# Wider fillers, earlier zeros and a new written order in a delta-rule and mixture-attention kernel

## The chip, the cores and the metric

The kernel runs on 1 core of one Trainium2 chip. The metric is the device time in microseconds (us); lower is better. The engines have short names: PE is TensorE (PEld its weight load), DVE is VectorE, ACT is ScalarE, POOL is GpSimd, SP is SyncE, which issues all transfers here.

## The reference

Two layers follow each other. The first is a linear recurrence (the delta rule) over 768 tokens for 4 x 8 heads of width 48; its output is the input of the second, four softmax-attention experts of width 64 with top-2 gating.

```python
k_n = k / (np.linalg.norm(k, axis=-1, keepdims=True) + 1e-06)
for t in range(S):
    kt, vt, bt = (k_n[:, :, t], v[:, :, t], beta[:, :, t, None])
    y[:, :, t] = np.einsum('bhd,bhde->bhe', q[:, :, t], state)
    v_old = np.einsum('bhde,bhd->bhe', state, kt)
    state = state + bt[:, :, :, None] * np.einsum('bhd,bhe->bhde', kt, vt - v_old)
...
for e in range(E):
    q = x @ wq[e]
    k = x @ wk[e]
    v = x @ wv[e]
    scores = scale * (q @ k.transpose(0, 2, 1))
    scores = np.where(causal, -1000000000.0, scores)
    a = softmax(scores)
    ye = a @ v @ wo[e]
    out += (weight of e for each token, 0 unless e is in its top 2) * ye
```

## The kernel before

The recurrence is done in blocks of 64 tokens. A chunk, numbered n from 0 to 5, holds two of the four batch entries, all heads and 256 tokens, in four parts c of 64 tokens; chunks 0 to 2 are one half of the batch from first to last token, chunks 3 to 5 the other. For each chunk the Gram matrices of its keys are formed (ga for chunks 0 to 2, gb for 3 to 5) and evacuated by ACT (ge, ad, ae, al). Norms are taken (nm), the blocks are turned round (bi), and a 32 x 32 triangular system is solved by substitution: chunk 0 on DVE (the steps s0.1 to s0.31), the others on POOL (sv.n.0 to sv.n.31; sv.n.32 is on DVE). bo and tn transpose the solution, m1, we, m2 and me join two solved halves into the inverse of a 64 x 64 block. Then the parts follow one after another, since each needs the state behind the one before: gk (products of keys with keys and state), xs (values less their old part, DVE), tx (solve), us (copies), ku (state update), se (the new state), yy (outputs), yh and yl (outputs split in two words). hx moves some rows of the outputs with six transfers. The second layer is made of pj, pv (projections), mx, mz, mr, mt, mo (row maxima), sc (scores), sm (mask), ex (exponentials), av (values), gt (gating), ra, rb, nr (normalising), ft and fo (output projection), oo and so (storing). It runs some chunks behind the recurrence, between its matmuls.

Nothing is scheduled by a compiler. The string ORDER is the program: each word is a step, with the numbers of its chunk and part behind dots and its accumulator banks behind "@", and every engine runs its own instructions of these words in that order. The words that load are lk (keys), lq (queries), lt and lv (keys and values by token), le (keys for the Gram matrices), lc (constants; lc.1 is beta), ww (weights, staged in one of two places and then split by wh on ACT and wl on POOL; the place is free for a later ww only when wl is done). SP issues them in the order of their words and waits in place where a buffer isn't free. vs scales the values by the norms on POOL.

fl.k is a filler: k matmuls on a tile of zeros, ZB, into a bank that nothing reads, so that PE is not idle while it waits. zb zeroes ZB. zz and zb also zero states and two banks. ex0 and sq0 are activations whose only use is that ACT switches its table there.

```python
for word in ORDER.split():
    word, _, at_ = word.partition("@")
    name, *a = word.split(".")
    ...
    steps[name](*a)
```

An fp32 matmul of the recurrence counts as two instructions on PE; a filler counts as one. Nearly all matmuls carry the line of the helper mm, L199, and nearly all copies on ACT that of copy, L201.

## Time and profile before

| | us |
|---|---|
| median of 3 runs | 426.77 (424.69 to 426.94) |
| profiled execution | 421.56 |
| its span | 419.8 |

| engine | busy us | share | instructions |
|---|---|---|---|
| PE | 399.7 | 95% | 9119 |
| DVE | 302.8 | 72% | 635 |
| ACT | 205.7 | 49% | 453 |
| POOL | 227.0 | 54% | 415 |

The times are those of whole runs; the span is the time from the first to the last instruction of the one execution that was profiled, and 1.76 us lie around it. Busy time counts fillers like any other matmul. In rows of the trace, the time behind an operation's start is the busy time of the group, xN is the number of instructions, and brackets tell how long the engine had been idle before it and what ended that.

### The profile page before, as it was taken

The numbers are of one execution on the slowest core, as the hardware profiler recorded it, in microseconds if no ns is written. First come the engines' busy times: TensorE is split into PE (matmuls) and PEld (weight loads), VectorE is DVE, ScalarE is ACT, GpSimd is POOL, SyncE is SP. The second block draws the span as 40 slices with busy tenths as digits, with TensorE's granted clock in tenths as the row PEclk, the third lists the DMA queues.
The fourth block names the chain that finished last, engine by engine and source line by source line (L and its number), as shares of the span: only waits on it lengthen the run. The fifth ranks groups of instructions, "written<-read, shape, count | busy, mean of one in ns | idle before, by whom it ended". The sixth has DMA issues, their size and how long they took to land.

```text
span 419.8 us, 20613 instructions
## 1 busy us (share of the span) xinstructions
PE 399.7 (95%) x9119; PEld 356.3 (85%) x9119; DVE 302.8 (72%) x635; ACT 205.7 (49%) x453; POOL 227.0 (54%) x415
## 2 busy tenths in 40 slices
...
GB/s 212 244 125 132 6 61 90 199 87 174 53 153 141 140 69 58 77 142 154 213 56 43 94 21 108 103 120 4 160 173 125 52 20 13 11 16 62 4 3 75
DMA packets 81657, 39.81 MB, mean 95 GB/s; under 512 B 64992, under 2 KB 74848, under 8 KB 81568
## 3 DMA queue, kind: packets, MB, share of 16 engines
...
q8 instruction: 71, 1.16, 1.1%
q14 instruction: 18, 0.15, 0.1%
...
## 4 chain that ended last, share of the span: by engine, by line
PE 73%; DVE 10%; DMA 8%; SPq 3%; issue 3%; ACT 1%; POOL 1%; DVEq 0%; ACTq 0%
PE p L199 71%; DMA bt<-in_beta_dram 2%; DVE p L460 2%; DMA qp<-in_kq_dram 2%; DVE vs L459 1%; SPq L637 1%; DVE mp L730 1%; DMA at<-in_wqk_dram 1%; PE p L814 1%; DVE qp L395 1%; DMA kv<-in_kv_dram 1%; DMA at<-in_wo_dram 1%; PE p L739 1%; DVE p L725 1%; POOL wl L312 1%
## 5 line engine op out<-in xcount | busy, mean ns | idle before, releaser
L508 POOL TENSOR_TENSOR tm<-b 128x30 f32<-128x30 f32 (+9 forms) x150 | 72.9, 486 | 28.9 <-DVE b L504 18.1
L510 POOL TENSOR_TENSOR b<-b,tm 128x30 f32<-128x30 f32 (+9 forms) x150 | 77.7, 518 | 11.8
L199 PE MATMUL p<-zb 128*128 128x128 bf16 x883 | 55.9, 222 | 4.5 <-DVE zb L316 3.3
L775 ACT ACTIVATE at<-p 128x768 f32<-128x768 f32 (+1 forms) x48 | 43.3, 917 | 31.4 <-PE p L199 14.8
L199 PEld LDWEIGHTS <-zb 128*128 128x128 bf16 x883 | 50.7, 99 | 6.5 <-DVE zb L316 3.3
L201 ACT ACTIVATE qp<-p 64x192 f32<-64x192 f32 (+1 forms) x92 | 36.9, 401 | 26.0 <-PE p L199 24.6
L730 DVE TENSOR_REDUCE mp<-p 128x2 f32<-128x1024 f32 (+3 forms) x40 | 44.4, 1115 | 2.9 <-PE p L199 1.9
L199 PE MATMUL p<-vs,at 128*64 128x65 f32 x1344 | 44.9, 223 | 0.9 <-ACT at L775 0.9
L199 PEld LDWEIGHTS p<-vs,at 128*64 128x64 f32 x1344 | 41.4, 137 | 4.4 <-issue 2.0
L395 DVE TENSOR_TENSOR qp<-p,cs 64x256 f32<-64x256 f32 x96 | 40.5, 421 | 5.8 <-PE p L199 4.1
L199 PE MATMUL p<-xu,wh 128*128 128x512 f32 (+1 forms) x168 | 40.3, 373 | 0.0
L572 POOL TENSOR_TENSOR kv<-kv,nt 128x384 f32<-128x384 f32 x24 | 19.6, 831 | 31.2 <-DMA kv<-in_kv_dram 25.7
L199 PEld LDWEIGHTS p<-xu,wh 128*128 128x128 f32 x168 | 27.8, 188 | 5.8 <-issue 0.5
L199 PE MATMUL p<-qh,kh 64*128 64x128 f32 (+1 forms) x192 | 29.1, 299 | 0.2 <-DVE mp L730 0.2
L199 PE MATMUL p<-qp 128*48 128x64 f32 (+1 forms) x768 | 26.3, 221 | 2.2 <-issue 1.9
L780 DVE TENSOR_TENSOR p<-p,km 128x512 f32<-128x512 f32 x24 | 16.6, 696 | 14.6 <-PE p L199 14.2
L199 PE MATMUL p<-qh,kl 64*128 64x128 f32 (+1 forms) x192 | 26.9, 276 | 0.0
L199 PE MATMUL p<-ql,kh 64*128 64x128 f32 (+1 forms) x192 | 26.9, 276 | 0.0
L199 PE MATMUL p<-wh,xu 128*128 128x260 f32 x144 | 26.3, 294 | 0.6 <-DVE mp L730 0.6
L199 PEld LDWEIGHTS p<-qp 128*48 128x48 f32 (+1 forms) x768 | 23.0, 123 | 4.5 <-issue 2.8
L199 PE MATMUL p<-mr,sl 64*128 64x128 f32 (+1 forms) x192 | 26.7, 274 | 0.0
L199 PE MATMUL p<-qp,kf 48*64 48x112 f32 (+1 forms) x768 | 23.8, 259 | 0.3 <-issue 0.3
...
## 6 DMA issues: line engine op xcount, KB each, us to landing
...
```

The source lines that it names most:

```text
L199: T.matmul(o, lhsT=a, rhs=b, start=start, stop=True, skip_group_check=True)
L201: copy = lambda o, a: S.activation(o, a, AF.Copy)
L312: G.tensor_tensor(flat(WL[w])[:, i:i + n], st(k)[:, 0:n], flat(WH[w])[:, i:i + n], op=OP.subtract)
L395: V.tensor_tensor(QP[zi(n, c) % RQ][tok(f), f, 4 * x:4 * x + 4, 0:64], gv(n, c)[r, x, :, 0:64], PMK[r, None, :].to_broadcast([64, 4, 64]), ...
L459: V.tensor_tensor(tv, t, l, op=OP.mult)
L460: V.tensor_tensor(PX[:, 0:i, i + 1:], PX[:, 0:i, i + 1:], tv, op=OP.subtract)
L508: G.tensor_tensor(tv, b[:, i:i + 1, i + 1:].to_broadcast([128, i, m]), b[:, 0:i, i:i + 1].to_broadcast([128, i, m]), op=OP.mult)
L510: G.tensor_tensor(b[:, 0:i, i + 1:], b[:, 0:i, i + 1:], tv, op=OP.subtract if n == 1 else OP.add)
L572: G.tensor_tensor(vt, vt, NRM[n % 2][:, c * NP:c * NP + NP, None].to_broadcast([128, NP, HD]), op=OP.mult)
L730: V.tensor_reduce(o[:, :, y0:y0 + per], g, axis=AXL.X, op=OP.max, negate=True)
L775: S.activation(at(n, b, y, kp)[:, :, 0:w], P8[:, b0:b0 + 2, 0:w], AF.Exp, scale=0.125)
L780: V.tensor_tensor(g, g, KM[:, None, None, :].to_broadcast([128, 2, 2, 128]), op=OP.add)
```

## The change

The string ORDER is another one, with the same steps in another sequence, and three things in the steps differ.

- ZB is 512 columns wide instead of 128. A second filler, fw.k, runs k matmuls of 512 columns; fl.k runs k of 128 as before. Counted in the two strings, there were 883 narrow fillers in 30 places and there are 272 narrow and 143 wide ones in 51 words. Before m1.0.0, 487 narrow ones become 57 narrow and 106 wide; behind it, 396 narrow become 215 narrow and 37 wide.
- Zeroing ZB is DVE's first instruction. The memsets of two banks are one, in a word of its own (zp), behind it.
- For chunks 3 to 5 the Gram blocks are addressed through hold(), which describes the same words of GF in rows of 256. (gs has the new name gps.)

The order was searched with another assumption on the time that blocks of the program take while transfers are queued; that search is not part of the kernel. Of the two orders only the lines that are spoken of are shown.

```diff
--- before
+++ after
-lk.0.2 zz.4 zz.0 lk.0.3 lk.0.1 lk.0.0 le.1.3 zz.2 zb le.1.1 zz.5 le.1.0 zz.1 sq0 lc.1 le.1.2 le.2.3 fl.24@3 ga.0.1.1@2
-lc.2 ga.0.1.0@3 al.1.1 ae.1.1.0 le.2.2 ga.0.0.1@4 ae.1.1.3 le.2.0 ae.1.0.0 ae.1.1.1 ae.1.0.1 lq.0.2 ga.0.0.0@5 al.0.1
-ae.1.0.3 ae.0.1.0 lt.0.2 ae.0.1.1 ae.0.0.0 lv.0.1 ae.0.1.3 ae.0.0.1 lt.0.0 ae.0.0.3 lq.0.0 al.1.0 bi.0 fl.25@6
...
-ad.1.1.0.3 ad.1.1.1.0 fl.59@7 ga.2.0.0@2 ad.1.0.0.3 ge.2.1.0 nm.0.3 a2.0 bi.1 ga.2.1.1@6 wh.0 ga.2.0.1@3 ge.2.0.0 s0.8
-gk.0.0@45 a2.1 ge.2.0.1 s0.9 s0.10 s0.11 wh.1 vs.0.0 nm.1.0 s0.12 vs.0.1 ge.2.1.1 nm.1.1 nm.1.2 s0.13 wl.0 s0.14
-sv.1.0 ww.2 gd.2 s0.15 s0.16 s0.17 sv.1.1 sv.1.2 s0.18 wh.2 sv.1.3 lv.0.2 s0.19 ex0 sv.1.4 s0.20 wl.2 s0.21 s0.22 wl.1
-s0.23 vs.0.2 ww.3 s0.24 lk.1.0 sv.1.5 lq.0.1 s0.25 s0.26 sv.1.6 ww.4 s0.27 sv.1.7 s0.28 wh.3 s0.29 sv.1.8 s0.30 s0.31
...
-sv.1.9 sv.1.10 bo.0 sv.1.11 tn.0 tc0.2.1 fl.379@7 m1.0.0@1 sv.1.12 tc0.0.0 m1.0.1@7 tc0.0.1 we.0.0 sv.1.13 we.0.1
-pm.0.0.0.0 fl.14@2 m2.0.0@1 pm.0.0.1.1 m2.0.1@7 pm.0.0.0.1 me.0.0.0 sv.1.14 nm.1.3 tc0.1.0 pm.0.0.1.0 me.0.0.1 tc0.1.1
...
-me.0.2.0 sv.1.27 we.0.3 fl.17@6 tx.0.2@45 sv.1.28 us.0.2.1 le.3.1 sv.1.29 us.0.2.0 le.3.0 lk.1.1 sv.1.30 fl.26@6
-yy.0.2@1 sv.1.31 ku.0.2 yh.0.2.0 yl.0.2.0 wl.3 m2.0.3@4 yh.0.2.1 pj.0.1.0.0@5 se.0.2.1 yl.0.2.1 pj.0.1.0.1 wl.4
-me.0.3.1 ww.5 pj.0.3.0.0@1 me.0.3.0 pj.0.1.0.2 zz.3 sv.1.32 se.0.2.0 ww.6 gb.3.0@23 lv.1.1 le.3.2 vs.1.0 bo.1 lk.1.2
-pv.0.0.1@4 ge.3.0.1 lt.1.0 vs.0.3 ge.3.0.0 pj.0.3.0.1 wh.5 pj.0.3.0.2 tn.1 gk.0.3@23 wl.5 kh.0.3.0 kh.0.1.0 wh.6
...
-lv.5.2 oo.3.1.1 lt.5.2 fl.6@2 ku.5.0 lv.5.1 lv.5.3 yy.5.0@1 se.5.0.0 so.3.1.0 so.3.1.1 pj.4.2.2.0@6 yh.5.0.0 lk.5.3
...
+lk.0.2 zz.4 zb lk.0.3 zp sq0 lk.0.1 lk.0.0 zz.0 lc.1 zz.2 le.1.2 zz.5 le.1.3 le.1.1 ww.0 le.1.0 fl.24@3 ga.0.1.1@2
+lt.0.1 le.2.2 ga.0.1.0@3 al.1.1 le.2.3 ae.1.1.0 le.2.0 ae.1.1.3 ae.1.0.0 lq.0.3 zz.1 ae.1.0.3 fl.12@5 ga.0.0.0@4
+al.1.0 ae.1.0.1 le.2.1 ga.0.0.1@5 lc.2 ae.1.1.1 ae.0.0.0 ae.0.0.1 ae.0.0.3 ae.0.1.0 al.0.0 lv.0.1 ae.0.1.1 lv.0.2
+ae.0.1.3 fw.3@6 fl.7@6 ga.1.1.1@2 lt.0.0 bi.0 lq.0.1 ge.1.1.1 lq.0.0 ad.1.1.1.1 nm.0.0 ad.1.1.1.3 wh.0 nm.0.1 fw.6@6
+fl.4@6 ga.1.0.1@4 px nm.0.2 ga.1.1.0@3 ad.1.0.1.0 ge.1.0.1 s0.1 ga.1.0.0@6 bs s0.2 al.0.1 ad.1.1.0.2 s0.3 ad.1.1.0.0
...
+vs.0.2 s0.12 nm.1.0 gd.2 nm.1.1 nm.1.2 wh.1 wl.2 s0.13 lq.0.2 s0.14 sv.1.0 s0.15 ww.4 s0.16 s0.17 sv.1.1 s0.18 vs.0.0
...
+s0.29 s0.30 s0.31 wl.1 sv.1.10 ww.3 bo.0 sv.1.11 tn.0 tc0.0.0 fw.90@7 fl.4@7 m1.0.0@1 vs.0.1 tc0.2.0 m1.0.1@4 sv.1.12
+m1.0.2@5 we.0.1 we.0.0 nm.1.3 tc0.0.1 fl.9@7 m2.0.0@1 sv.1.13 me.0.0.1 tc0.1.0 sv.1.14 tc0.1.1 me.0.0.0 we.0.2 fw.6@7
+fl.7@7 tx.0.0@23 sv.1.15 m2.0.1@1 us.0.0.1 gk.0.0@45 me.0.1.1 us.0.0.0 sv.1.16 me.0.1.0 lk.1.0 pm.0.0.0.0 tc0.3.1
+fl.4@7 ku.0.0 pm.0.0.1.1 wh.4 pm.0.0.1.0 sv.1.17 m1.0.3@1 se.0.0.0 pm.0.0.0.1 se.0.0.1 we.0.3 fl.10@7 gk.0.1@23
+sv.1.18 ex0 xs.0.1 sv.1.19 pm.0.1.1.1 fw.2@7 fl.5@7 tx.0.1@45 pm.0.1.1.0 pm.0.1.0.0 yy.0.0@1 sv.1.20 pm.0.1.0.1
+us.0.1.0 lq.1.0 bi.2 us.0.1.1 wl.4 tc0.2.1 sv.1.21 fw.3@7 fl.7@7 yy.0.1@4 lk.1.1 yh.0.0.0 lv.1.0 yh.0.0.1 m2.0.3@5
+le.3.1 yl.0.0.1 yh.0.1.0 sv.1.22 yl.0.0.0 ku.0.1 yh.0.1.1 yl.0.1.1 yl.0.1.0 m2.0.2@1 sv.1.23 se.0.1.0 hx.0.0 se.0.1.1
+me.0.2.0 sv.1.24 fl.10@7 gk.0.2@23 tc0.3.0 me.0.2.1 sv.1.25 wh.3 xs.0.2 pm.0.2.0.0 sv.1.26 fw.2@4 fl.5@4 tx.0.2@67
+pm.0.2.1.1 pm.0.2.0.1 le.3.0 us.0.2.1 sv.1.27 pm.0.2.1.0 ww.6 me.0.3.1 us.0.2.0 lv.0.3 sv.1.28 lt.1.0 fw.5@4 fl.7@4
+yy.0.2@1 le.3.2 sv.1.29 lv.1.1 sv.1.30 ku.0.2 lq.1.1 yh.0.2.1 yh.0.2.0 sv.1.31 gb.3.0@23 yl.0.2.1 yl.0.2.0 lq.1.2 wh.6
+me.0.3.0 wl.3 se.0.2.0 pj.0.1.0.0@4 lt.1.1 ge.3.0.0 se.0.2.1 sv.1.32 ww.5 fl.11@6 pv.0.0.1@1 ge.3.0.1 lt.0.3
+pj.0.1.0.1 bo.1 vs.1.1 lg.0.0.1 pj.0.3.0.0@5 pj.0.1.0.2 zz.3 pj.0.3.0.1 wl.6 ve.0.0.1 pj.0.3.0.2 pj.0.2.0.0@1 vs.1.0
...
+gt.3.5 yh.4.1.0 sc.3.1.1.0@23 rb.3.0 gt.3.6 xs.4.2 nr.3.0 yl.4.1.0 lv.5.1 sm.3.1.1 hx.4.0 fl.9@1 tx.4.2@67 sv.5.28
...
@@ -244,7 +245,7 @@
     CS, QM = sb("cs", 209), sb("qm", 128)
     SL = sb("sl", 2, 128, dt=F32R)
     BT = sb("bt", NU, 32)
-    ZB = sb("zb", 128, dt=BF16)
+    ZB = sb("zb", 512, dt=BF16)
     IDN, PMK, LOW, H16 = CS[:, 0:128], CS[:, 128:192], CS[:, 192:208], CS[:, 208:209]
     KM, Z0, HF = sb("km", 128), sb("zr", 32), sb("hf", 1)
     VF = VS.rearrange("p a b c d -> p (a b c d)")
@@ -259,6 +260,9 @@
     PX = P8[:, 0:2].rearrange("p a b -> p (a b)").rearrange("p (j i) -> p j i", i=32)
     AD = AT[0].rearrange("p a b -> p (a b)").rearrange("p (t i) -> p t i", i=32)
 
+    def hold(n, k):
+        return GF[n % RG][:, 16 * k:16 * k + 16].rearrange("p (m t) s -> p m (t s)", m=4)
+
     def zi(n, c):
         return 4 * n + c
 
@@ -314,7 +318,9 @@
 
     def zb():
         V.memset(ZB, 0.0)
-        V.memset(P8[:, 7], 0.0)
+
+    def zp():
+        V.memset(P8[:, 6:8], 0.0)
 
     def ex0():
         S.activation(RS[0][:, 0, 0:1], ZB[:, 0:1], AF.Exp)
@@ -324,8 +330,6 @@
 
     def zz(k):
         if k < 2:
-            if k == 0:
-                V.memset(P8[:, 6], 0.0)
             for i in (k, k + 2):
                 V.memset(zs(i), 0.0)
         elif k == 2:
@@ -343,10 +347,18 @@
 
     def fl(k):
         for _ in range(k):
-            mm(P8[:, BK["fl", k][0], 0:128], ZB, ZB)
+            mm(P8[:, BK["fl", k][0], 0:128], ZB[:, 0:128], ZB[:, 0:128])
+
+    def fw(k):
+        for _ in range(k):
+            mm(P8[:, BK["fw", k][0], 0:512], ZB[:, 0:128], ZB)
 
 
     def le(n, c):
+        if n > 2:
+            nc.sync.dma_start(hold(n, c // 2)[0:112, 2 * (c % 2):2 * (c % 2) + 2],
+                              kq[n, c, 0:112, 0:512].rearrange("p (a b) -> p a b", a=2))
+            return
         nc.sync.dma_start(GF[n % RG][0:112, NP * c:NP * c + NP], kq[n, c, 0:112, 0:512].rearrange("p (a b) -> p a b", a=NP))
 
     def ga(n, k, x):
@@ -362,13 +374,13 @@
     def gb(n, k):
         b = BK["gb", n, k][0]
         for j in range(2):
-            a = GF[n % RG][:, NP * (2 * k + j):NP * (2 * k + j) + NP]
             for i in range(4):
                 for x, f in TURN:
                     p, o = 4 * x + i, 256 * j + 64 * i
-                    mm(P8[gr(f, p), b + x, o:o + 64], a[feat(f), p], a[feat(f), p])
-
-    def gs(n, k, x):
+                    a = hold(n, k)[feat(f), 2 * j + x, 64 * i:64 * i + 64]
+                    mm(P8[gr(f, p), b + x, o:o + 64], a, a)
+
+    def gps(n, k, x):
         g = P8[:, BK["gb", n, k][0] + x] if n > 2 else bank(("ga", n, k, x))
         return g.rearrange("p (c i j) -> p c i j", c=2, i=4)
 
@@ -376,7 +388,10 @@
         return a.rearrange("p (c x i) j -> p c x i j", x=2, i=4)[:, 2 * k:2 * k + 2, x]
 
     def ge(n, k, x):
-        copy(half(GF[n % RG], k, x), gs(n, k, x))
+        if n > 2:
+            copy(hold(n, k).rearrange("p (c x) (i j) -> p c x i j", x=2, i=4)[:, :, x], gps(n, k, x))
+            return
+        copy(half(GF[n % RG], k, x), gps(n, k, x))
 
     def gk(n, c):
         b, a, q = BK["gk", n, c][0], KF[zi(n, c) % RK], QP[zi(n, c) % RQ]
...
```

## Rows read from the trace of the kernel before

**Rows 1.** The page: busy time of each engine with its share of the span and its instructions, and the engines' shares of the chain of work that ended last.
```profile
PE 399.7 (95%) x9119; PEld 356.3 (85%) x9119; DVE 302.8 (72%) x635; ACT 205.7 (49%) x453; POOL 227.0 (54%) x415
...
PE 73%; DVE 10%; DMA 8%; SPq 3%; issue 3%; ACT 1%; POOL 1%; DVEq 0%; ACTq 0%
```

**Rows 2.** Busy time of each engine in two stretches, cut where m1.0.0 starts. Columns: stretch, its length, then busy us and instructions of PE, PEld, DVE, ACT and POOL, the granted clock of PE, the share of the transfer engines and GB/s.
```profile
0.00:46.90 46.90, 41.76 (x905) 40.59 (x905) 37.83 (x94) 18.04 (x39) 32.44 (x53) 1.00 0.64 160
46.90:416.50 369.60, 357.97 (x8216) 315.71 (x8216) 264.98 (x542) 187.15 (x415) 194.60 (x363) 1.00 0.34 86
```

**Rows 3.** The same two stretches for the instructions alone that read or write ZB: PE, PEld, DVE, ACT.
```profile
0.00:46.90 46.90, 29.29 (x487) 28.34 (x487) 0.11 (x1) 0.41 (x2) 1.00 0.64 160
46.90:416.50 369.60, 26.60 (x396) 22.34 (x396) 0.00 (x0) 0.00 (x0) 1.00 0.34 86
```

**Rows 4.** The timeline of the opening: DVE's first memsets, PE's first groups, and the time to landing of the four key loads (min, median, max).
```profile
1.00 0.48 DVE L328 MEMSET p<- 128x512 f32 x1 [1.00 <-PEq L893]
1.64 1.50 DVE L330 MEMSET qp<- 128x768 f32 x2 [0.15 <-issue]
3.10 0.11 DVE L316 MEMSET zb<- 128x64 uint32 x1
...
3.27 2.74 PE L199 MATMUL p<-zb 128*128 128x128 bf16 x24 [3.27 <-DVE zb L316]
5.94 4.54 PE L199 MATMUL p<-kf 48*64 48x64 f32 x128
...
0.82 1.81 SPq L272 DMA_DIRECT2D kf<-in_kq_dram  x4
...
DMA to landing us min/median/max: 2.9/4.0/5.1
```

**Rows 5.** The timeline of DVE, ACT and PE up to m1.0.0: the transpose that opens the first solve, the copy and the square root ahead of DVE's wait, the last transpose (bo.0), the long filler and m1.0.0.
```profile
11.85 1.97 DVE L442 STREAM_TRANSPOSE vs<-at 128x1024 f32<-128x1024 f32 x1 [0.29 <-ACT at L201]
...
26.51 0.63 ACT L201 ACTIVATE wh<-at 128x512 fp32r<-128x512 f32 x1 [0.80 <-DMA at<-in_wqk_dram]
27.05 0.34 ACT L424 ACTIVATE g<-b,hf 128x32 f32<-128x32 f32 x1
...
27.41 0.35 DVE L415 RECIPROCAL rr<-g 128x32 f32<-128x32 f32 x1 [0.39 <-ACT g L424]
...
44.58 2.25 DVE L467 STREAM_TRANSPOSE gf<-vs 128x1024 f32<-128x1024 f32 x1
...
25.14 21.33 PE L199 MATMUL p<-zb 128*128 128x128 bf16 x379
46.89 0.50 PE L199 MATMUL p<-gf,os 32*32 32x32 f32 x19 [0.41 <-DVE gf L467]
```

**Rows 6.** The timeline of POOL's first solve (its first and last instruction), DVE's second transpose behind it, the Gram block gb.3.0 on PE, and m1.1.0 on PE.
```profile
29.48 2.38 POOL L502 TENSOR_TENSOR b<-b,aa 128x1024 f32<-128x1024 f32 x1 [1.49 <-DVE aa L436]
...
69.82 1.27 POOL L512 TENSOR_SCALAR_AFFINE_SELECT b<-b 128x1024 f32<-128x1024 f32 x1
...
76.34 1.92 DVE L470 STREAM_TRANSPOSE tn<-b 128x1024 f32<-128x1024 f32 x1
...
72.97 1.16 PE L199 MATMUL p<-gf 48*64 48x64 f32 x64 [0.96 <-DMA gf<-in_kq_dram]
...
78.98 0.21 PE L199 MATMUL p<-dg,gf 32*32 32x32 f32 x1 [0.83 <-ACT vs L201]
```

**Rows 7.** Whom PE waited for from 46.9 to 416.5 us: total us, times, longest.
```profile
PE p L199 <- issue: 4.6, 5, 1.9
PE p L199 <- ACT at L775: 1.2, 2, 0.9
PE p L199 <- DMA gf<-in_kq_dram: 1.0, 1, 1.0
```

**Rows 8.** The instruction queue on the page (packets, MB, share), and the timeline of PE around its three longest idle times that are put down to "issue".
```profile
q8 instruction: 71, 1.16, 1.1%
...
19.06 2.74 PE L199 MATMUL p<-zb 128*128 128x128 bf16 x46 [1.19 <-issue]
...
105.19 1.00 PE L199 MATMUL p<-qp,kf 48*64 48x112 f32 x32
106.01 0.28 PE L199 MATMUL p<-gf 48*64 48x64 f32 x4
108.01 0.58 PE L199 MATMUL p<-gf 48*64 48x64 f32 x25 [1.72 <-issue]
...
313.32 0.44 PE L199 MATMUL p<-qp 128*48 128x64 f32 x9 [1.92 <-issue]
```

**Rows 9.** The timeline of SP, POOL and PE around the values of chunk 5.
```profile
320.03 1.95 SPq L281 DMA_DIRECT2D kv<-in_kv_dram  x4
...
325.45 0.83 POOL L572 TENSOR_TENSOR kv<-kv,nt 128x384 f32<-128x384 f32 x1 [12.96 <-DMA kv<-in_kv_dram]
...
326.93 0.49 PE L199 MATMUL p<-x,gf 64*64 64x48 f32 x17 [0.79 <-DVE x L575]
```

**Rows 10.** The timeline of ACT: the table switch of ex0, its activation, and a copy of the first recurrence steps with the idle time before it.
```profile
31.51 1.28 ACT L320 ACT_TABLE_LOAD   x1
32.80 0.20 ACT L320 ACTIVATE rs<-zb 128x1 f32<-128x1 bf16 x1
...
57.29 0.28 ACT L201 ACTIVATE h<-p 112x128 fp32r<-112x128 f32 x1 [2.05 <-PE p L199]
```

258 lines of the change are left out of this document (127 added, 131 removed).

## Prediction, made before the changed kernel was run

> **What bounds the kernel now.** The page comes first: TensorE (PE) is busy for 95% of the span, and 73% of the chain that ended last is PE [rows 1]. But 883 of its 9119 matmuls are fillers on zeros, so "busy" is not "useful". The table by stretches cuts the run at 46.9 us, where m1.0.0 starts and the first state can be updated [rows 2], and the same table for the filler operand alone separates the padding [rows 3]. Before the cut PE does 384 useful matmuls and 487 fillers, plus gk.0.0: the pace there is set elsewhere. After it, 369.6 us pass of which PE is busy 357.97, so it idles 11.63 us, and it holds 396 fillers. One filler costs 56 ns when they follow each other: 379 take 21.33 us [rows 5]. So the 396 cost 22.3 us of PE's line. What remains, 369.6 - 11.6 - 22.3 = 335.7 us, is useful matmul work, which the change neither adds to nor takes from; only its order differs. That gives the frame for the sum: the end moves by what the start of m1.0.0 moves, by what the fillers behind it shrink, and by what PE's idle time behind it changes.
>
> The opening shows who sets m1.0.0. VectorE (DVE) runs the 31 steps of the first triangular solve, ends them with the transpose at 44.58 + 2.25 us, and PE, done with 379 fillers, waits 0.41 us for it [rows 5]. GpSimd (POOL) runs the second solve from 29.48 us to the select that ends at 71.1; DVE then needs until 78.3 for the two transposes, and m1.1.0 starts at 78.98 [rows 6]. From there to the end I take PE as the pace setter, with short waits: the list of PE's waits behind 46.9 us names 4.6 us "issue" (nothing that the profile shows), 1.2 for ScalarE's (ACT) exponentials, 1.0 for a transfer [rows 7].
>
> **Edit 1, zeros first.** Today two memsets stand ahead of the one that fillers read: it starts at 3.10 us, and PE's first filler at 3.27 [rows 4]. In the new order it is DVE's first instruction, at about 1.00. It writes four times as much: between 0.11 us (the old one) and 0.44 (four times that), at a time when DVE later sits idle anyway. PE then starts 1.8 to 2.1 us earlier, and its 24 fillers, 2.67 us from first to the next group's start, end near 4.0 instead of 5.94. The first Gram blocks cannot use all of that: they need the first two of four key loads, which land 2.9 to 5.1 us after issue from 0.82 us on [rows 4], so they start at 4.2 to 5.3. Twelve new fillers inside the group take back 0.7 us at 56 ns or 1.3 at the 110 ns of the first fillers, and one state memset, zz.1 (1.5 us, as the pair in [rows 4]), now stands between DVE's copies. Gain at the transpose that starts the solve (11.85 us now): 0 to 0.9 us, I take 0.5.
>
> Further on, DVE idles 0.39 us for the square root of chunk 1, which on ACT queues behind a weight copy that waits for its load [rows 5]. In the new order another copy, wh.2, stands there, with a load issued earlier: 0 to 0.39, I take 0.39. m1.0.0 comes 0.9 us earlier (0 to 1.3). Behind it the POOL solve starts on DVE's result as well, idle 1.49 us for it today [rows 6], so it moves along; its interruptions (vs.0.0, wl.1, vs.0.1, wl.4 against wl.2, wl.1, vs.0.2 before) are nearly equal. **-0.9 us.** The total of zeroed words in the accumulators is unchanged, and the activation-table switch ex0 (1.28 us plus a 0.20 us activation) moves from idle time into the first recurrence steps. There ACT idles 2.05 us at a time today [rows 10], which covers it; uncovered it costs 1.5.
>
> **Edit 2, wide fillers.** Counted in the two orders: before m1.0.0, 487 narrow become 57 narrow and 106 wide; behind it, 396 narrow become 215 narrow and 37 wide. No row shows a wide one. Its bounds: 213 ns (512 columns at the 2.4 GHz level that the 56 ns spacing belongs to) and 225 (four narrow ones). Behind the cut: 215 x 0.0563 + 37 x 0.213 to 0.225 = 20.0 to 20.4 against 22.3 us. **-2.1 us**, if the gaps that they fill have become shorter; if PE must wait there all the same, 0. Ahead of the cut, 90 wide and 4 narrow take 19.4 us in place of 379 narrow (21.3); gk.0.0 has left too. PE's end of fillers there costs nothing while DVE's solve is later, and it would have to start past 26 us (25.14 now) to be late.
>
> **Edit 3, the order.** Useful matmul work between like milestones is the same within 2 us in both orders; what moves are neighbours, loads and copies. Three waits of today lose their cause in the text of the new order. gb.3.0 waits 0.96 us for keys [rows 6]; le.3.1 now precedes the six hx transfers and gb.3.0 follows yy.0.2. m1.1.0 waits 0.83 us for an ACT copy that queued behind a late weight load; that load, ww.6, needed POOL's wl.4, which now runs inside the solve instead of behind it. And PE waits 0.79 us at 326.93 because POOL waited 12.96 us for values issued at 320 [rows 9]; lv.5.1 is now issued before tx.4.2, a stage earlier. Together 2.6 us. But a new order has waits of its own that nobody foresaw, as these three were unforeseen: I take half, **-1.3 us** (-2.6 to +2.6).
>
> **Blocks of the program.** The instruction queue moved 71 packets, 1.16 MB [rows 8], which is 64 bytes for each of PE's 18238 matmuls and weight loads, or one packet for 128 pairs. PE stops inside dense runs for "issue": 1.72 us at 108, 1.92 at 313, and 1.19 in the opening, hidden there by the solve. The Trainium skill (Runtime: NRT & Kernel Launch, Instruction fetch mechanics) says that crossing from one block to the next is mostly hidden; the trace agrees for most of the 71 and disagrees at these places; by the rule this term would be 0 and the time 422.5. Behind the cut 4.6 us are at stake. 468 fewer matmuls alone give 3.7 blocks fewer, 5%, some 0.2 us; an order that places its gaps there could save up to 4.6; one that packs the dense runs closer could lose. I take a third, **-1.5 us** (-4.6 to +6). The rewriting of GF into hold() addresses the same words: 0, and it moves nothing.
>
> **Sum.** -0.9 - 2.1 - 1.3 - 1.5 = -5.8 us. The profiled execution took 421.56 us (span 419.8 and 1.76 around it): 415.8. The median of the runs shown is 426.77, 5.2 above; I carry the difference over unchanged: **421.0 us**, 1.4% faster. About 0.5% (2.1 us) is what a measurement of this kernel can tell from no change.
>
> **Rivals.** (a) The fillers shrink but the gaps don't: other engines set the pace there, PE idles instead, and blocks and waits come back elsewhere. For it: DVE is 72% busy and POOL nearly full up to 300 us. Against it: PE is the chain for 73%. Only the opening's 0.9 remains: 425.9.
>
> (b) Slower: late program blocks. Behind the cut 144 filler instructions of 396 are gone, each of which had given the fetch 56 ns; dense runs (32 matmuls in 1.0 us at 105.2) follow each other more closely. Each late block costs 1.7 to 1.9 us [rows 8]. Without the block term the sum is -4.3, so it decides from four more late blocks on: -4.3 + 4 x 1.8 = +2.9, 429.7. For it: all boundaries fall anew. Against it: only two such stops stand in 370 us today.
>
> (c) PE idles ahead of m1.0.0. If the last Gram blocks end as early as 22.8 us (PE starts earlier and gk.0.0 is gone), the wide fillers end at 42.2, and 3.8 us of idleness follow until about 46. The first 24 fillers ran at 110 ns and later ones at 56 [rows 4, 5], that is at the lower and at the higher of the two clock levels, although the clock column says 1.00 throughout. The whole slow start cost 24 x 0.054 + about 0.8 us in the Gram blocks, 2.1 us; once more, that makes 423.1. The longest idle stretch behind which the rows show PE unslowed is 1.92 us. The Trainium skill (TensorE: Matmul & The Clock Gate, Part 1) says that the array returns to the lower level after idling; no run here shows it yet.
>
> **Chances.** As summed 0.53; (a) 0.22; (b) 0.13; (c) 0.12. The first spreads over 417.5 to 424.6 and counts as faster but for 0.01; (c) is 0.08 faster and 0.04 same; (a) 0.20 same and 0.02 slower; (b) 0.12 slower, 0.01 same. Faster 0.60, same 0.26, slower 0.14. The range 415.5 to 429 takes in (a), (c) and the lower half of (b): 415.5 is the sum with all block stops gone and the full 2.6 us; above 429 lies about 0.07.
>
> **What would show it.** The first filler near 1.3 us; m1.0.0 near 46.0; filler time behind it near 20 us; PE idle behind it near 9 us, with no stop of 1.7 us for "issue"; no wait of PE for keys at gb.3.0, nor for values of chunk 5. Wrong it is if m1.0.0 comes no earlier, if PE's idle time behind the cut grows by what the fillers shrank (a), if "issue" passes 10 us (b), or if narrow fillers or small matmuls behind m1.0.0 are spaced at twice their present distance (c).

## The result: slightly slower, and the profile after

The changed kernel took 427.24 us (median of 20 runs, 423.4 to 430.5); the kernel before, run beside it on the same chip, took 424.86 (20 runs). The ratio is 1.0086, with a 95% interval of 1.0064 to 1.0107; this ratio and those below are of the runs that count as fast, while the two medians of all 20 would give 1.0056. Timed again later beside other kernels it was 1.0042 (1.0004 to 1.0081). The forecast was 421.0 us and faster; the time lies inside its range of 415.5 to 429, on the other side of "before" than its likeliest case.

The page of the kernel after, to set beside [rows 1] and [rows 8]: span, busy times, the granted clock in 40 slices, the instruction queue, the chain that ended last.

```profile
span 425.7 us, 19696 instructions
...
PE 404.8 (95%) x8651; PEld 341.1 (80%) x8651; DVE 301.2 (71%) x634; ACT 206.1 (48%) x453; POOL 224.4 (53%) x415
...
PEclk9999699999999999996999999999999899999999
...
q8 instruction: 68, 1.11, 1.1%
...
PE 72%; DVE 12%; DMA 5%; SPq 4%; issue 3%; ACT 1%; POOL 1%; DVEq 0%; ACTq 0%; POOLq 0%
```

PE has 468 matmuls fewer and is busy for 5 us longer. The clock row shows where: three dips, in slices where the execution of before has 1.00 [rows 2]. The table by stretches, cut at m1.0.0 as [rows 2] is, then the three stretches in which the granted clock was 0.50 (the lower of its two levels, 1.2 GHz; 1.00 is the upper one, 2.4 GHz):

```profile
0.00:45.54 45.54, 39.60 (x548) 25.89 (x548) 38.14 (x93) 16.11 (x36) 32.59 (x54) 1.00 0.65 159
45.54:422.40 376.86, 365.25 (x8104) 315.21 (x8104) 263.02 (x542) 189.58 (x418) 191.85 (x362) 0.98 0.34 85
45.53:52.36 6.83, 6.82 (x142) 5.16 (x143) 1.79 (x2) 3.60 (x10) 6.08 (x10) 0.50 0.01 2
195.72:202.55 6.83, 5.53 (x57) 5.46 (x57) 4.40 (x14) 1.16 (x4) 1.61 (x6) 0.50 0.32 60
328.84:332.25 3.41, 3.41 (x34) 2.37 (x37) 2.26 (x6) 0.60 (x1) 0.66 (x1) 0.50 0.85 236
```

Against [rows 2]: m1.0.0 comes 1.35 us earlier, and the work behind it takes 376.86 - 369.60 = 7.26 us more. That is 365.25 - 357.97 = 7.28 more busy time; the idle time, 376.86 - 365.25 = 11.61, is what it was (11.63). In the three stretches PE was busy for 6.82 + 5.53 + 3.41 = 15.76 us at half speed, which at 1.00 would have been some 7.9 us by the two levels. So the additional busy time is about what the half clock took, and whatever the fillers gave was spent with it. The same two stretches for the operand of the fillers, against [rows 3]:

```profile
0.00:45.54 45.54, 28.33 (x163) 14.72 (x163) 0.27 (x1) 0.20 (x1) 1.00 0.65 159
45.54:422.40 376.86, 26.63 (x252) 16.53 (x252) 0.00 (x0) 0.20 (x1) 0.98 0.34 85
```

252 fillers took as long as 396 had (26.60). The timeline of DVE and PE up to m1.0.0, and the word tx.0.0 behind it (kv,gf), against [rows 4, 5]; the last two lines are m1.0.0 with m1.0.1, 32 matmuls each, and tx.0.0 in the kernel before:

```profile
0.94 0.27 DVE L320 MEMSET zb<- 128x256 uint32 x1 [0.94 <-PEq L908]
...
1.27 2.74 PE L200 MATMUL p<-zb 128*128 128x128 bf16 x24 [1.27 <-DVE zb L320]
3.94 2.19 PE L200 MATMUL p<-kf 48*64 48x64 f32 x64
...
7.43 1.91 PE L200 MATMUL p<-kf 48*64 48x64 f32 x64 [0.53 <-DMA kf<-in_kq_dram]
...
21.57 19.82 PE L200 MATMUL p<-zb 128*128 128x512 bf16 x94
45.54 1.92 PE L200 MATMUL p<-gf,os 32*32 32x32 f32 x64 [4.14 <-DVE gf L482]
...
53.09 0.68 PE L200 MATMUL p<-kv,gf 64*64 64x48 f32 x32
...
46.89 1.20 PE L199 MATMUL p<-gf,os 32*32 32x32 f32 x64 [0.41 <-DVE gf L467]
...
51.03 0.68 PE L199 MATMUL p<-kv,gf 64*64 64x48 f32 x32
```

The zeros were early and so was PE: the long filler began at 21.57 (25.14 before) and ended at 41.4. DVE's solve came 1.3 us earlier only. PE stood idle for 4.14 us, and the 64 matmuls of m1.0.0 and m1.0.1 then took 1.92 us instead of 1.20. From m1.0.0 to tx.0.0 it took 7.55 us.

Whom PE waited for behind the cut, against [rows 7], and the four stops above 1.1 us there:

```profile
PE p L200 <- issue: 5.4, 5, 3.2
PE p L200 <- DVE gf L482: 4.1, 1, 4.1
PE p L200 <- DMA xu<-h: 2.1, 2, 1.5
PE p L200 <- ACT wt L202: 1.3, 1, 1.3
```

```profile
82.97 0.68 PE L200 MATMUL p<-x,gf 64*64 64x48 f32 x32 [1.27 <-ACT wt L202]
...
197.03 0.21 PE L200 MATMUL p<-dg,gf 32*32 32x32 f32 x1 [3.24 <-issue]
...
314.91 0.18 PE L200 MATMUL p<-tn,gf 32*32 32x32 f32 x1 [1.20 <-issue]
...
327.38 0.50 PE L200 MATMUL p<-xu,wh 128*128 128x512 f32 x1 [1.54 <-DMA xu<-h]
```

The row of 4.1 us for DVE is the wait ahead of m1.0.0, which ends at the cut; the idle time behind it is the rest. The stop of 3.24 us stands in m1.3.1 (dg,gf), a run of 64 matmuls some 10 ns apart, 25 of them ahead of it, and the second fall of the clock lies on it. What SP had queued just ahead of it, and how busy the transfer engines were (second last column of the last line):

```profile
190.05 0.63 SPq L285 DMA_DIRECT2D kv<-in_kv_dram  x1
190.78 0.37 SPq L359 DMA_DIRECT2D gf<-in_kq_dram  x1
191.25 0.39 SPq L847 DMA_DIRECT2D out_dram<-ot  x1
191.68 0.42 SPq L285 DMA_DIRECT2D kv<-in_kv_dram  x1
192.20 0.39 SPq L847 DMA_DIRECT2D out_dram<-ot  x1
192.64 0.46 SPq L276 DMA_DIRECT2D kf<-in_kq_dram  x1
```

```profile
190.00:195.80 5.80, 3.58 (x144) 3.15 (x132) 5.59 (x11) 2.92 (x8) 0.83 (x1) 0.99 0.91 254
```

Six transfers in 2.6 us, a share of 0.91, and one 16 KB packet of the instruction queue in the midst of them: it began at 193.88 us, 0.1 us after PE had stopped, and took 1.8 us; PE went on 1.35 us after its end.

### The profile page after: what moved, and what is told of

It is laid out like the page before. It is cut to its first block, busy times and chain, and to the rows that moved or that the text cites. A ratio compares the mean times of both kernels' runs of the same rounds, so it can differ in the third digit from the quotient of the medians.

```text
span 425.7 us, 19696 instructions
## 1 busy us (share of the span) xinstructions
PE 404.8 (95%) x8651; PEld 341.1 (80%) x8651; DVE 301.2 (71%) x634; ACT 206.1 (48%) x453; POOL 224.4 (53%) x415
## 4 chain that ended last, share of the span: by engine, by line
PE 72%; DVE 12%; DMA 5%; SPq 4%; issue 3%; ACT 1%; POOL 1%; DVEq 0%; ACTq 0%; POOLq 0%
PE p L200 70%; SPq L652 3%; DVE p L475 2%; DMA xu<-h 2%; DVE vs L474 2%; DMA kf<-in_kq_dram 1%; PE p L829 1%; DMA at<-in_wo_dram 1%; PE p L754 1%; DVE mp L745 1%; DVE qp L410 1%; SPq L847 1%; DMA gf<-in_kq_dram 1%; DVE dg L482 1%; DVE gf L482 1%
## 5 line engine op out<-in xcount | busy, mean ns | idle before, releaser
L200 PE MATMUL p<-zb 128*128 128x128 bf16 (+1 forms) x415 | 55.0, 285 | 1.3 <-DVE zb L320 1.3
L200 PEld LDWEIGHTS <-zb 128*128 128x128 bf16 x415 | 31.2, 102 | 21.4 <-issue 1.7
L200 PE MATMUL p<-xu,wh 128*128 128x512 f32 (+1 forms) x168 | 41.8, 377 | 2.1 <-DMA xu<-h 2.1
L610 DVE COPY qp<-p 64x192 f32<-64x192 f32 x48 | 17.0, 354 | 16.5 <-PE p L200 15.5
L200 PE MATMUL p<-wh,xu 128*128 128x260 f32 x144 | 27.2, 302 | 0.1
```

The source lines that it names most:

```text
L200: T.matmul(o, lhsT=a, rhs=b, start=start, stop=True, skip_group_check=True)
L610: V.tensor_copy(o, a)
```

## The experiments

The theory was: the idle time ahead of m1.0.0 lets the clock fall and costs more than the whole gain (G), and a program block that arrives late in a dense run while transfers are queued does the same once more (B). The rivals: the new order is slow in itself; the wide fillers are slow; the zeros do it. All ratios are to the kernel before, on the same chip, with a 95% interval.

| kernel | what it is | ratio |
|---|---|---|
| after | the change | 1.0086 (1.0064 to 1.0107) |
| e11_changed_again | the same, timed beside e9 and e10 | 1.0042 (1.0004 to 1.0081) |
| e1_gap_filled | after, idle time ahead of m1.0.0 filled | 0.9978 (0.9945 to 1.0010) |
| e2_loads_spread | after, three loads moved behind m2.3.1 | 1.0035 (1.0006 to 1.0064) |
| e3_both | e1 and e2 | 0.9958 (0.9924 to 0.9993) |
| e4_before_short | before, with a shorter long filler | 1.0195 (1.0156 to 1.0233) |
| e5_old_order_zeros_first | old order, zeros first | 0.9965 (0.9929 to 1.0000) |
| e6_narrow_only | e1, all fillers narrow | 1.0032 (0.9996 to 1.0069) |
| e7_blocks_shifted | e3, 63 instructions more ahead of m1.0.0 | 0.9956 (0.9916 to 0.9995) |
| e8_gram_first | e3, one projection behind gk.5.1 | 0.9936 (0.9897 to 0.9974) |
| e9_half_filled | e8, 2.4 us of idle time ahead of m1.0.0 again | 1.0003 (0.9973 to 1.0034) |
| e10_best_narrow | e8, all fillers narrow | 1.0085 (1.0046 to 1.0124) |
| e12_narrow_timed | e10, 26 narrow fillers less | 1.0009 (0.9976 to 1.0042) |

**The idle time filled (e1).** The kernel after with 17 more wide fillers ahead of m1.0.0; five wide and two narrow ones in place of 24 narrow keep the later boundaries of the program where they were.

```diff
-zz.5 le.1.3 le.1.1 ww.0 le.1.0 fl.24@3 ga.0.1.1@2
+zz.5 le.1.3 le.1.1 ww.0 le.1.0 fw.5@3 fl.2@3 ga.0.1.1@2
-tn.0 tc0.0.0 fw.90@7 fl.4@7 m1.0.0@1
+tn.0 tc0.0.0 fw.107@7 fl.4@7 m1.0.0@1
```

> The changed kernel, with the one long stretch of fillers ahead of m1.0.0 made 17 wide fillers longer (fw.90 becomes fw.107, some 3.7 us), and 17 fewer filler instructions in the opening (24 narrow become 5 wide and 2 narrow), so that every later matmul keeps its place among the blocks of the program. Theory 1, the clock falls because PE stands idle 4.14 us ahead of m1.0.0: the clock column stays 1.00 behind m1.0.0 (it was 0.5 from 45.5 to 52.4 us), tx.0.0 comes about 3 us earlier (50 instead of 53.1), and if that reaches the end the ratio to the kernel before falls from 1.009 to about 1.001; m1.0.0 itself stays near 45.5. Rival, the lost time there has another cause (waits of the new order): tx.0.0 stays near 53 and the ratio near 1.009. A third way: tx.0.0 comes earlier but the second solve on POOL sets m1.1.0, and only about 1 us is left at the end (1.006).

It gave 0.9978: 1.1% or 4.6 us back against the first ratio of the kernel after, 2.7 us against its second (the comparisons were made apart, and each ratio is known to some 0.3%). In the profiled execution a stop of 1.64 us in the opening made PE late, so that the fillers outlasted the solve and m1.0.0 came at 47.93 and tx.0.0 at 52.75, other than the text says; but from one to the other it took 4.82 us instead of 7.55, and the end lay 2.4 us ahead of that of the kernel after. Behind m1.0.0 the clock stayed at 1.00 up to 199.1 us, where it fell for 3.41 us behind a stop of 2.71 us in m1.3.1.

**Three loads moved (e2), and both edits (e3).**

```diff
-us.2.3.1 le.5.3 pm.2.3.0.1
+us.2.3.1 pm.2.3.0.1
...
-we.3.0 lt.3.1 us.2.3.0
+we.3.0 us.2.3.0
...
-m2.3.0@45 lk.3.1 bi.4
+m2.3.0@45 bi.4
...
-m2.3.1@45 oo.1.1.1
+m2.3.1@45 le.5.3 lt.3.1 lk.3.1 oo.1.1.1
```

> The changed kernel with three of the six transfers that are issued between 190.0 and 193.1 us (le.5.3, lt.3.1, lk.3.1, 640 KB of 1216) moved behind m2.3.1, that is behind the stop of PE at 193.8 to 197.0. Theory 2, that stop is the fetch of a program block that waits behind queued transfers (its packet starts at 193.9, when PE already stands): the stop shrinks from 3.2 us to under 1, the clock does not fall at 195.7, and m2.3.1 comes about 4 us earlier against the kernel before (+1 instead of +5.1); the ratio falls from 1.009 to about 1.001 if it reaches the end. Rival, the stop has nothing to do with the queue (the block is asked for too late by PE's own pace): stop and clock stay, ratio near 1.009, or slower by the later loads.

> Both edits, the longer filler ahead of m1.0.0 and the three transfers moved. If both theories hold and both losses reach the end, the sum: 3 + 4 us less than the changed kernel, ratio to the kernel before about 0.993. If only one reaches the end, about 1.001. If neither, 1.009.

e2 gave 1.0035. Its profile has the stop in m1.3.1 at 1.87 us instead of 3.24 and no fall behind it; the text expected under 1 us. The gap ahead of m1.0.0 (4.15) and the fall there are still present, and another fall follows a stop of 2.04 us at 110. e3 gave 0.9958. Two lines of its timeline: m1.0.0 after 0.73 us of waiting, and the stop in m1.3.1, still 2.36 us, behind which the clock fell for 3.41 us.

```profile
45.36 1.20 PE L198 MATMUL p<-gf,os 32*32 32x32 f32 x64 [0.73 <-DVE gf L480]
...
194.30 0.18 PE L198 MATMUL p<-dg,gf 32*32 32x32 f32 x1 [2.36 <-issue]
```

e2 and e3 were timed on one chip in one session and differ only in the fillers ahead of m1.0.0: 1.0035 (1.0006 to 1.0064) against 0.9958 (0.9924 to 0.9993). That 0.8%, known to some 0.4%, is the cleanest price of the gap in the new order.

Moving the loads shortens the stop in the dense run; it does not take it away. One profile each would not show it, since the unaltered kernel gave 3.24 and 2.40 us (e11). But the three profiles that have the stop with the loads unmoved (after, e1, e11) show 2.40 to 3.24 us, and the five with them moved (e2, e3, e7, e8, e9) 1.27 to 2.36. The packets of the instruction queue in the traces tell how. In these eight and in e4 below PE goes on 1.1 to 1.5 us after the end of a packet. With the loads unmoved, that packet begins 0.10 to 0.21 us after PE has stopped (0.71 in e4); with them moved, 0.44 to 1.05 us before. During the stops of e2, e3, e8 and e9 the transfer engines had a share of 0.00 to 0.03. So here the queued transfers went with a later packet and a longer stop, and a stop was left when they were moved, as the rival in the text of e2 had it in part. What the move is worth in time, 0.005 at e2 and 0.002 between e1 and e3, is within the intervals.

**The same mistake made in the old order (e4).** The kernel before with a long filler that ends as early as that of the kernel after.

```diff
-bo.0 sv.1.11 tn.0 tc0.2.1 fl.379@7 m1.0.0@1
+bo.0 sv.1.11 tn.0 tc0.2.1 fl.305@7 m1.0.0@1
```

> The kernel before, with 74 fillers fewer ahead of m1.0.0 (fl.379 becomes fl.305), so that PE stands idle 4.6 us there in place of 0.4. Nothing else is changed; m1.0.0 waits for the same transpose. Theory 1: the clock falls to 0.5 at about m1.0.0 for some 7 us, tx.0.0 comes about 3 us later (54 instead of 51.0), and the end 1 to 3 us later (ratio 1.002 to 1.007). Rival: clock stays 1.00 and the time is that of the kernel before, but for program blocks that lie 74 matmuls earlier (up to 2 us either way).

It is the strongest result: 1.0195, from 74 instructions taken out of a place where they delay nothing. The timeline at m1.0.0, at tx.0.0 and in m1.3.1, then two of its three stretches at 0.50:

```profile
46.09 1.92 PE L198 MATMUL p<-gf,os 32*32 32x32 f32 x64 [4.12 <-DVE gf L466]
...
53.21 1.11 PE L198 MATMUL p<-kv,gf 64*64 64x48 f32 x32
...
199.75 0.20 PE L198 MATMUL p<-dg,gf 32*32 32x32 f32 x1 [3.06 <-issue]
```

```profile
44.24:54.48 10.24, 8.39 (x199) 7.78 (x200) 5.64 (x8) 3.65 (x10) 9.06 (x16) 0.50 0.02 4
197.84:204.67 6.83, 4.92 (x35) 4.85 (x35) 3.87 (x12) 1.76 (x5) 2.12 (x7) 0.50 0.31 56
```

The old order, the old narrow fillers and the old zeros do the same as the new ones once PE idles 4.1 us here: the 64 matmuls take 1.92 us, and tx.0.0 comes 2.18 us later than before although m1.0.0 came 0.80 earlier. And since the whole program behind lies 74 instructions further ahead in its blocks, a boundary now falls into m1.3.1 and PE stops for 3.06 us, where the kernel before had at most 0.41 nearby. (Both kernels stop behind the same 350 and 2640 matmuls of their counts, with other words at the second.) The third fall, at 112.5 for 3.41 us, follows a stop of 1.21 us. The end came 8.3 us later by the ratio and not 1 to 3, as the text expected: the two stops at boundaries and the falls behind them come on top of the gap. Both G and B are thus seen without the new order, in one kernel; their shares of 1.0195 are not separated.

**Zeros first alone (e5).** The old order; only the zeros and the memset of two banks are moved, and the tile and the Gram addressing are those of the kernel after.

```diff
-lk.0.2 zz.4 zz.0 lk.0.3 lk.0.1 lk.0.0 le.1.3 zz.2 zb le.1.1 zz.5
+lk.0.2 zz.4 zb zp zz.0 lk.0.3 lk.0.1 lk.0.0 le.1.3 zz.2 le.1.1 zz.5
```

> The order of the kernel before, fillers narrow as there, with the zeros written first (zb moved to DVE's front, the bank memsets behind it in one). The only part of the change that is in it is the first. If the opening gains by itself: first filler at 1.3 us, bo.0 some 0.5 to 1 us earlier than 44.6, and the 379 fillers end about 2 us earlier, so PE stands idle some 1.5 us ahead of m1.0.0. Theory 1 (only a long idle time lets the clock fall): clock stays 1.00 behind m1.0.0, ratio 0.998 to 1.000. Rival: 1.5 us are enough, the clock falls there and the ratio is 1.005 or more.

The ratio was 0.9965, at the edge of no change, and the median of all its runs (424.38 us) is that of the kernel before beside it (424.53). No gain reached m1.0.0. The timeline of PE in its opening:

```profile
1.27 2.74 PE L198 MATMUL p<-zb 128*128 128x128 bf16 x24 [1.27 <-DVE zb L318]
...
7.27 1.91 PE L198 MATMUL p<-kf 48*64 48x64 f32 x64 [1.12 <-DMA kf<-in_kq_dram]
...
11.37 1.44 PE L198 MATMUL p<-gf 48*64 48x64 f32 x46 [0.69 <-DMA gf<-in_kq_dram]
...
18.53 2.74 PE L198 MATMUL p<-zb 128*128 128x128 bf16 x46 [0.97 <-issue]
...
47.00 1.20 PE L198 MATMUL p<-gf,os 32*32 32x32 f32 x64
```

PE began 2.0 us earlier and gave it back in waits for the key loads and in stops for "issue". No gap arose ahead of m1.0.0, so that neither the theory nor the rival of the text was put to the test. The 1.35 us that the profile of the kernel after gained at m1.0.0 did not come with the zeros alone. How far they belong to the order of its opening is open: in e11, the same kernel, m1.0.0 came at 46.84, 0.05 us earlier than before. The transpose that ends the solve starts between 42.90 and 45.29 us in the eleven profiles of that opening (median 43.96), and at 43.83, 44.53 and 44.58 in the three of the old one.

**Narrow fillers in the filled order (e6).** e1 with every wide filler replaced by narrow ones of about its time (408 for the 107 ahead of m1.0.0).

```diff
-tn.0 tc0.0.0 fw.107@7 fl.4@7 m1.0.0@1
+tn.0 tc0.0.0 fl.408@7 fl.4@7 m1.0.0@1
```

> The changed kernel with the long stretch ahead of m1.0.0 filled, but every wide filler replaced by four narrow ones (408 narrow ahead of m1.0.0). It tells what the width of the fillers is worth: the time in fillers behind m1.0.0 is 0.4 us longer by the rate (56 ns for 128 columns against 215 for 512), and there are some 430 more matmuls, 3.4 blocks of the program. If width matters only through the rate, the ratio is that of the wide version, 0.998 within 0.002. If the additional blocks cost, it is 1.002 or more. If wide fillers themselves let the clock fall (fewer weight loads), the clock column here would be 1.00 where the wide version had falls.

It gave 1.0032 against 0.9978 for e1, with 477 matmuls more; the intervals touch, so that 0.005 is not settled. In its profile the clock fell too, for 3.41 us behind a stop of 2.38 us at 312: the falls do not belong to wide fillers.

**Boundaries shifted (e7), and a projection moved (e8).** Both start from e3; e7 first.

```diff
-tc0.0.0 fw.107@7 fl.4@7 m1.0.0@1
+tc0.0.0 fw.86@7 fl.88@7 m1.0.0@1
```

```diff
-se.5.0.1 pj.4.2.2.0@5 lt.5.2
+se.5.0.1 lt.5.2
...
-gk.5.1@23 oo.3.1.1
+gk.5.1@23 pj.4.2.2.0@5 oo.3.1.1
```

> The version with the stretch filled and the three transfers moved, with 21 of its wide fillers ahead of m1.0.0 replaced by 84 narrow ones: same time there (4.7 against 4.5 us), but every later matmul lies 63 places further on among the blocks of the program, half a block. If the stop of 2.4 us at 191.9 is set by where a block ends in the dense run of m1 and m2, it shrinks under 1 us or moves to another place, and other stops change too; the ratio then moves by 0.003 or more either way from 0.996. If it is set by the queued transfers alone, the stop stays within 0.5 us of 2.4 at the same words, and the ratio stays 0.996.

> The version with the stretch filled and the three transfers moved, with one more word moved: pj.4.2.2.0, which stands and waits for the transfers of hx.4.1 (0.73 us there, 1.54 in the changed kernel), now comes behind gk.5.1, which does not need them. If that wait is on the path of the recurrence, it goes and xs.5.1 comes 0.7 us earlier, ratio 0.994; if it only moves, 0.996.

In e7 63 more instructions stand ahead of the words of m1.3.1, and the stop stays at the same place in the count, behind 4295 matmuls, as in the kernel after and in e8, but now in other words, those of m2.3.0: it belongs to the boundary and not to the words. It was 1.43 us there; other stops, of 1.6 and 2.4 us with a fall each, appeared at 80 and 315 us, and the ratio, 0.9956, is that of e3. In e8 the Gram work of gk.5.1 no longer stands behind a projection that waits for xu, and the wait (0.73 us in e3, 1.54 in the kernel after) is gone. But xs.5.1 comes at 323.56 us, in e3 at 323.58: the 0.7 us of the text did not come there, and 0.9936 against 0.9958 is within the intervals. It has the best ratio, and beats both kernels. Its timeline at m1.0.0 and tx.0.0, and its table behind the cut:

```profile
23.04 23.49 PE L198 MATMUL p<-zb 128*128 128x512 bf16 x111
46.53 1.20 PE L198 MATMUL p<-gf,os 32*32 32x32 f32 x64
...
51.34 0.68 PE L198 MATMUL p<-kv,gf 64*64 64x48 f32 x32
```

```profile
46.53:415.00 368.47, 358.58 (x8104) 310.25 (x8104) 264.64 (x542) 189.58 (x418) 191.15 (x362) 1.00 0.34 87
```

No gap, 64 matmuls in 1.20 us, and 4.81 us from m1.0.0 to tx.0.0, where the kernel after took 7.55: the half clock costs 2.7 us there. (The kernel before took 4.14; the new order has m1.0.2 there in place of m2.0.1, and 0.7 us more of fillers.)

**The gap put back, shorter (e9), the narrow best (e10), the change again (e11).** e9 and e10 start from e8; e11 is the kernel after, unaltered. The edit of e9 puts eleven narrow fillers, not two as its text says, in place of two wide ones in the opening, so that the count of instructions stays. Of e10 the main edit is shown: every other fw.k became fl.4k (fl.22 for the first fw.5). The "columns as before" of its text does not hold for the long one, which was matched by its time.

```diff
-ww.0 le.1.0 fw.5@3 fl.2@3 ga.0.1.1@2
+ww.0 le.1.0 fw.3@3 fl.13@3 ga.0.1.1@2
...
-tc0.0.0 fw.107@7 fl.4@7 m1.0.0@1
+tc0.0.0 fw.98@7 fl.4@7 m1.0.0@1
```

```diff
-tc0.0.0 fw.107@7 fl.4@7 m1.0.0@1
+tc0.0.0 fl.408@7 fl.4@7 m1.0.0@1
```

> The best order so far (e8) with nine 512-column fillers less behind the opening, and two narrow ones for two wide in the opening, so that TensorE stands idle for about 2.4 us ahead of m1.0.0 instead of 0.5. Theory 'idle ahead of m1.0.0 costs by its length': the granted clock stays at 1.00 behind m1.0.0, tx.0.0 within 0.5 us of that of e8, ratio 0.992 to 0.997. Rival 'any idle of more than 2 us here is followed by the half clock': 0.5 granted behind m1.0.0, tx.0.0 some 2 to 3.4 us later, ratio 1.000 to 1.006.

> The best order (e8) with each 512-column filler written as four of 128, columns as before, some 300 instructions more. Theory 'width only saves instructions and what the fetch of their blocks costs': ratio 0.994 to 1.000, the difference to e8 0.003 to 0.006, in stops that fall at other matmuls. Rival 'width is worth nothing': ratio within 0.002 of e8's, about 0.994.

> The changed kernel unaltered, on the chip of these runs, for the comparison with them. If the loss belongs to the kernel: ratio 1.006 to 1.011, and 4 us of idle ahead of m1.0.0 with 0.5 granted behind it again. If it belonged to the chip of the first timing: ratio below 1.003.

e9 lost nearly all that e8 had won: 1.0003. Its timeline, and the stretch at 0.50:

```profile
23.79 21.32 PE L198 MATMUL p<-zb 128*128 128x512 bf16 x100 [0.16 <-issue]
47.54 1.70 PE L198 MATMUL p<-gf,os 32*32 32x32 f32 x64 [2.43 <-DVE gf L480]
...
55.17 0.68 PE L198 MATMUL p<-kv,gf 64*64 64x48 f32 x32
```

```profile
47.90:54.73 6.83, 6.50 (x133) 4.85 (x128) 1.45 (x2) 3.25 (x10) 6.04 (x11) 0.50 0.01 2
```

2.43 us of idle time, then 6.83 us at half speed, and 7.63 us from m1.0.0 to tx.0.0 against 4.81: 2.8 us, near the difference of the two ratios (0.0067 x 424 = 2.8, with intervals that just touch). So it is not the length of the gap that costs but the fall behind it, and a gap of 2.4 us costs as much as one of 4.1. The theory as written, that a gap this short costs by its length, failed; the rival's 2 to 3.4 us for tx.0.0 held (2.8, counted from m1.0.0) and its ratio, 1.000 to 1.006, too.

e11 gave 1.0042, between the two ranges of its text. Its profiled execution is another than the first: a stop of 1.37 us at 19.6 and a fall behind it delayed PE in the opening, the gap was 1.81 us, and no fall followed it. Its timeline at m1.0.0 and tx.0.0:

```profile
46.84 1.20 PE L200 MATMUL p<-gf,os 32*32 32x32 f32 x64 [1.81 <-DVE gf L482]
...
51.66 0.68 PE L200 MATMUL p<-kv,gf 64*64 64x48 f32 x32
```

From one to the other it took 4.82 us: the same program took 7.55 us there with the fall and 4.82 without. Falls of 3.41 us followed stops of 1.89 (ACT, at 80.7), 2.40 (in m1.3.1) and 1.78 us (at 314) instead, and the mean clock was 0.984 against 0.978. How often the clock is lost is told by the mean granted clock of the timed executions. One stretch of 3.41 us at 0.50 takes 0.004 from it, one of 6.83 us 0.008, so that 0.994 has room for the first and not for the second:

| kernel | executions | mean clock: lowest, median, highest | with 0.994 or more |
|---|---|---|---|
| before (four comparisons) | 108 | 0.979, 0.992, 1.000 | 48 |
| after and e11 | 32 | 0.978, 0.984, 0.992 | 0 |
| e2 | 12 | 0.978, 0.990, 0.992 | 0 |
| e4 | 6 | 0.972, 0.978, 0.984 | 0 |
| e9 | 12 | 0.978, 0.988, 0.992 | 0 |
| e1 | 12 | 0.987, 0.995, 0.999 | 7 |
| e3 | 12 | 0.987, 0.994, 1.000 | 7 |
| e5 | 12 | 0.986, 0.992, 0.999 | 3 |
| e6 | 12 | 0.975, 0.993, 0.999 | 6 |
| e7 | 12 | 0.991, 0.996, 1.000 | 9 |
| e8 | 10 | 0.986, 0.996, 1.000 | 9 |
| e10 | 12 | 0.980, 0.992, 0.996 | 5 |
| e12 | 12 | 0.976, 0.994, 0.999 | 6 |

None of the 62 executions of the kernels that leave a gap ahead of m1.0.0 (after, e11, e2, e4, e9) has 0.994 or more; of the others 100 of 202 have. The 48 executions of before with the higher clock have a median of 423.0 us, the other 60 of 425.7.

**Width by itself (e10, e12).** e10 gave 1.0085 against 0.9936 for e8. But 408 narrow fillers, which began late behind two stops in the opening, outlasted the solve by 1.7 us. e12 has 382 in that place.

```diff
-tc0.0.0 fl.408@7 fl.4@7 m1.0.0@1
+tc0.0.0 fl.382@7 fl.4@7 m1.0.0@1
```

> As the narrow version of the best order (e10), whose 408 narrow fillers behind the opening ended 1.7 us after the solve did, but with 382 of them, which at 56 ns take the 21.5 us that 102 wide ones of 211 ns take. If the time that e10 lost to e8 (1.0085 against 0.9936) is the overshoot at m1.0.0: m1.0.0 within 0.6 us of the end of the solve as in e8, ratio 0.994 to 0.999. If it is what some 300 more instructions cost where their blocks are fetched: m1.0.0 as in e8 and the ratio still 1.002 to 1.008, with the loss at stops behind it.

(That text counts 102 wide fillers; e8 has 107 and 4 narrow in that place. They took 23.49 us, and less 0.23 for the narrow ones that is 0.217 us for a wide one, not 0.211.) e12 gave 1.0009, between the two ranges. In its profile m1.0.0 came at 46.66, 0.13 us behind e8, and tx.0.0 4.81 us later, as in e8. The rest lies at stops further on: 2.69 us at 70.2, which the profile puts down to a load, and 2.54 at 315.7 for "issue", each with a fall behind it:

```profile
73.41:76.82 3.41, 3.41 (x60) 3.20 (x52) 3.41 (x2) 2.51 (x6) 0.66 (x1) 0.50 0.92 231
319.17:322.58 3.41, 3.41 (x50) 2.69 (x52) 0.00 (x0) 1.20 (x3) 0.00 (x0) 0.50 0.24 54
```

So of the 0.015 that e10 lost to e8, 0.008 went with 26 fillers (the overshoot of 1.7 us is 0.004 of that; the rest is within the intervals), and 0.007 remains for narrow fillers. e12 has 451 matmuls more than e8, not some 300. Whether the 0.007 is their own cost or the place at which they put the boundaries is not settled; the two stops point to the second, and neither range of the text held. The comparison crosses chips and sessions, but narrow fillers were nowhere faster.

## Why the prediction was wrong, step by step

**The step that failed** is the sentence on the wide fillers ahead of the cut, "PE's end of fillers there costs nothing while DVE's solve is later". The filler's early end itself was foreseen: 42.2 and 3.8 us of idleness in rival (c), against 41.4 and 4.14. The wait did cost nothing. What followed did: 6.83 us at half clock, 2.7 us at tx.0.0, and 0.8% of the time between e2 and e3. Rival (c) named this and gave it 0.12, because the only work at the lower clock that the rows showed was the start [rows 4], and the longest stop behind it, 1.92 us, had no fall after it. Its price of 2.1 us was near for the place (2.7). But it was charged against a sum of -5.8, and that sum did not come.

**Blocks of the program**: -1.5 us taken, from a bound of -4.6 to +6. The 68 packets were as counted, but "issue" behind the cut rose from 4.6 to 5.4 us, with one stop of 3.24 us, where the longest had been 1.92. To that comes its fall: 5.53 us busy at half clock, 2.8 us. The count of blocks told little; what mattered is where a boundary falls and how late its packet begins. e4 shows the first with nothing else changed behind m1.0.0: 74 instructions fewer, and a stop of 3.06 us in m1.3.1. The Trainium skill (Runtime: NRT & Kernel Launch, Instruction fetch mechanics) calls the crossing of a block mostly hidden; the trace agrees for most of the 68, and disagrees at a boundary in a dense run of small matmuls: 3.24, 3.06 and 2.71 us with transfers queued ahead of it (after, e4, e1), 1.27 and 1.45 us with fewer (e9, e8).

**Edit 1**: m1.0.0 near 46.0 was predicted, 45.54 measured, and the first filler at 1.27 (about 1.3). That the time fits is in part luck: with the zeros alone (e5) m1.0.0 stayed at 47.00, and the same kernel had it at 46.84 in its second profile (e11).

**Edit 2**: -2.1 us behind the cut, from 22.3 to 20.0 or 20.4. By the view of [rows 3] the fillers of the kernel after took 26.63 us, no less than 26.60, since those behind m1.0.0 ran at half clock. In e8, where the clock was 1.00 throughout, the same view gives 25.18 for the same 252 fillers. So the term was of the right sign, came to 1.4 us of 2.1 by this view, and was not paid out in the kernel after.

**Edit 3**: of the three waits, the one at gb.3.0 shrank from 0.96 to 0.55 us. Behind m1.1.0 ACT is still waited for (1.27 us at 82.97; 1.97 and 1.89 in e1 and e11). POOL still waits for values (10.89 us at 327.88), but PE no longer waits for it there; another wait came at the same place, 1.54 us for xu, which the new order issued later. PE's idle time behind the cut was to be near 9 us and was 11.61. Taking half was still too much.

**What was to show it wrong**: "if narrow fillers or small matmuls behind m1.0.0 are spaced at twice their present distance (c)". The 64 matmuls in 1.92 us instead of 1.20, at half the granted clock, are that sign.

**The base of the sum** was flattering too. The profiled execution of before had 1.00 throughout, and I read that as the kernel's nature. Over 108 executions its median is 0.992: the old order loses some clock in more than half of them, and the medians of the two groups lie 2.7 us apart. The median of three runs that the sum carried over, 426.77, was high by chance as well: the 20 that include them have 424.86.

**The frame and smaller slips.** The frame took the useful matmul work behind the cut as unchanged. But the 32 matmuls of gk.0.0 moved from ahead of the cut to behind it (8216 - 396 = 7820 useful ones before, 8104 - 252 = 7852 after), which is 0.6 us. The lower end of the range, by its own terms, is 416.6 and not 415.5. And POOL was not nearly full up to 300 us: it was busy for 5.06 and 5.47 of 20 us from 180 and from 240 on. Neither of the last two decides anything.

**What stays open.** e8 has what the sum asked for: no fall, m1.0.0 0.36 us earlier, idle time behind the cut 368.47 - 358.58 = 9.89 (1.74 less), and fillers that take 1.4 us less. That makes -3.5; the span is 1.8 us shorter. Of the 1.7 us between, gk.0.0 is 0.6; no run here shows where the rest of the useful work takes longer. Why the ratio of the kernel after was 1.0086 once and 1.0042 later is not shown either. The worth of e2's and e8's moves by themselves (0.2% each on top of e1) is not resolved either.
